# Row loads on one queue, one store on another, and the last inverse step's copies shared differently

## The chip, the cores and the metric

The kernel runs on one core of a Trainium2 chip. The metric is the time of one execution on the device, in microseconds (us), lower being better. Several executions are timed; the figure is their median. One further execution is taken with the hardware profiler and gives the profile and the trace.

The core has five engines that run their own instruction streams: TensorE (PE, matmuls into PSUM; PEld is its weight load), VectorE (DVE), ScalarE (ACT), GpSimd (POOL) and SyncE (SP, which here only issues DMAs). DMAs can be issued by SyncE, ScalarE and GpSimd, each into a queue of its own, in the order of the issuing engine's program. Engines wait for one another, and for DMAs, on semaphores.

## The reference

Two layers of each kind, with residuals. Layer A mixes tokens and channels by a filter in the 2D Fourier domain; layer B is a two-matrix MLP with Mish.

```python
def _A_ref(x, w_r, w_i):                      # x: 1 x 2048 x 1024
    X = rfft2(x.astype(float32)); X = X * (w_r + 1j * w_i)
    return irfft2(X, s=(S, D)).astype(bfloat16)

def _B_ref(x, w1, b1, w2):                    # w1: 1024 x 3584, w2: 3584 x 1024
    h = x @ w1 + b1
    return (h * tanh(softplus(h))) @ w2

x = x + _A_ref(_layernorm(x), A_w_r, A_w_i)
x = x + _B_ref(_layernorm(x), B_w1, B_b1, B_w2)
x = x + _A_ref(_layernorm(x), A_w_r, A_w_i)
x = x + _B_ref(_layernorm(x), B_w1, B_b1, B_w2)
```

## The kernel before

The program is written out by hand: Python functions append instructions to one list per engine, in the order in which they are called, and a small tracker adds the semaphore waits that reads and writes of named resources demand. There is no planner: the order of the calls is the order of each engine's work, and an instruction that waits holds back everything behind it on its engine.

x lies in SBUF as XS, 16 tiles of 128 tokens by 1024 channels. Layer A does the Fourier transforms as steps of matmuls with constant tables: two forward steps over short factors (`s1` L626, matmuls L641; `s2` L740, matmuls L748), a third along the tokens (`s3`), the filter's multiplication on VectorE, and back through `i1`, `i2` and `i4`. The work between `s2` and `i2` goes in eight groups g = 0 to 7, interleaved by a written-out order (`order_A`).

**The start.** The prologue loads x twice: as XS, for the statistics of the layer norm, and in another arrangement, XR, which `s1` multiplies. XR is filled by `rows` (L404): for each q of four quarters (32 of 128 positions n1) and each of eight channel blocks h, one DMA of 512 rows of 256 bytes, 128 KB. SyncE issues all of quarters 0 and 2 and the even h of quarters 1 and 3 (24 loads). The odd h of quarter 1 are issued by GpSimd, after a wait for all of quarter 0. The odd h of quarter 3 are issued by ScalarE from `late_rows`, called in `first_scales` (L596) after the statistics. Behind the rows SyncE issues the table FD, which `s2` needs, the small table JT, and then (`open_tables`, `constants`) the first filter weights w_r and w_i, the further tables and M, BD, MT and others. The layer norm's scales are folded into the tables of `s1`: `scaled` (L611) makes 16 scaled tables, on ScalarE for j = 1 (L616), on GpSimd for j = 2, 4, 9, 10, 11 and 13, on VectorE for the rest (L622). `s1` runs 16 groups j of eight matmuls; j waits for quarter j // 4 of XR and for its scaled table; three pairs of PSUM banks take turns; the results are copied to SBUF by ScalarE (L647), and by VectorE for j = 5, 10 and 14 (L649). Then follow `s2` of group 0, the matmuls that mirror the filter's weights (L1039, which wait for JT, w_r and w_i of the group) and VectorE's copies of them (L1050), and `s2` of group 1, part of which VectorE copies (L785).

**The turn through memory.** After `i2` of a group, its result U (512 KB) is stored to a scratch tensor u_d in device memory (`u_turn`, L925) and read back with another arrangement into UT (`u_back`, L949, 2,048 rows of 256 bytes), because `i4` needs the groups interleaved over the partitions. SyncE issues the stores of groups 0 to 6 and the loads. Each load waits for its store. In SyncE's order `u_back(5)` stands before the store of group 6, and `u_back(6)` is issued during group 7. Group 7 is stored in two halves by ScalarE, and read back in four quarters (`u_last`, L955), two by ScalarE and two by SyncE. Meanwhile TensorE does some filler matmuls (`spin`, L658), puts the residual into the banks (`residual_first`, L1067) and does more filler (`hold`, L663: 16 matmuls in the first layer A, 11 in the second).

**The last inverse step.** `i4` (L1072, matmuls L1078) first does the token tiles 0 to 3, in four parts u of 32 channel positions, two banks each. `out_first(u, t, prog)` (L1083) copies the tiles t and t + 1 of part u from PSUM to XS, one instruction of 128 x 512 elements; the line shown for it is that of a helper (L579 on ScalarE, L583 on VectorE). It names its two banks as written, so two copies of the same part are made one after the other. After the copy of t = 0, VectorE takes a quarter of the statistics of tiles 0 and 1 (`stats_quarter`, L488); after u = 3 the quarters are aggregated (L490), and the scale follows (`root`, L448 on ScalarE and L450 on VectorE), the normalized tiles (`apply`, L528), their transposes on TensorE (L1188), copies (L1193) and the first matmuls of layer B (L1227). The order, in `layer_B`:

```python
for u in range(4):
    self.i4(0, 4, 32 * u, 32, 2 * u)
    if u == 0:
        self.hold(2, 7)
    self.out_first(u, 0, act)
    for j in range(2):
        self.stats_quarter(j, u)
    if u == 0:
        self.out_first(0, 2, dve)
```

The copies of t = 2 of u = 1, 2 and 3 follow on ScalarE. Both layers A end this way. Layer B computes its products by a scheme with seven instead of eight block products and takes most of the time (L1267, L1366); the change does not touch it.

Of the kernel before, what the change touches and what calls it, by code (L numbers as in the profile page):

```python
# [7 lines left out]
P = 128  # L8
# [172 lines left out]
class KB:  # L181
# [200 lines left out]
    def prologue(self):  # L382
        sp = self.sp
        self.op(self.pool, lambda e: e.memset(self.EPS[:], 1e-5), writes=[self.r_eps, self.r_warm])
        xt = self.x[0].rearrange("(t p) d -> p t d", p=P)

        for a, b in ((10, 11), (0, 1), (1, 2), (11, 12), (2, 3), (3, 4), (12, 13), (4, 6), (13, 14), (6, 8), (14, 15), (8, 10), (15, 16)):
            self.dma(self.act if a == 10 else sp, self.XS[:, a:b, :], xt[:, a:b, :], f"x{a}", writes=self.r_xs[a:b])
        self.warm(ACT.Sqrt)
        small = {}  # L390
        def load_small(name, n, d):
            b = self.alloc(name, self.o[name], [n], d)
            self.dma(sp, b.ap, self.con[name], name.lower(), writes=[b.res])
            small[name] = b
        load_small("M0", P, BF)
        load_small("IDF", P, F32)
        self.M0, self.IDF = small["M0"], small["IDF"]

        self.XR = self.alloc("XR", self.o["XR"], [P, P])
        self.r_xr = []  # L400
        xv = self.x[0].rearrange("(n2 n1) (h l) -> h n2 n1 l", n2=16, l=P)
        self.r_xr = [Res(f"xr{q}") for q in range(4)]

        def rows(q, h, prog):  # L404
            self.dma(prog, self.XR.ap[h:P:8, 32 * q:32 * q + 32, :], xv[h][:, 32 * q:32 * q + 32, :], f"xr{q}{prog.name}",
                     parts=[self.r_xr[q]], reads=self.r_xr[:1] if prog is self.pool else [])
        for q in range(4):
            for h in range(8):
                if h % 2 == 0 or q not in (1, 3):
                    rows(q, h, sp)  # L410
                elif q == 1:
                    rows(q, h, self.pool)
        self.late_rows = lambda: [rows(3, h, self.act) for h in (1, 3, 5, 7)]
        self.dma(sp, self.FD[:], self.con["FD"], "fd", writes=[self.r_fd])
        load_small("JT", 4 * P, BF)
        self.JT, self.r_jt = small["JT"].ap, small["JT"].res
        self.w1_next = 0
# [168 lines left out]
    def first_scales(self):  # L586


        dve, act = self.dve, self.act
        for j in range(10):  # L590
            self.stats_dve(j)
        for j in range(10, 16):
            self.stats_act(j)
        self.sums_to_mv(10, 6)
        self.root(0, 16)
        self.late_rows()  # L596
        rt = self.alloc("RT", self.o["RT"], [16, 8], F32)
        self.op(dve, lambda e: e.tensor_copy(rt.ap, self.RS[:, 2, :].unsqueeze(2).to_broadcast([P, 16, 8])),
                reads=self.r_rs, writes=[rt.res])
        bank = self.r_bank[7]  # L600
        self.group([lambda e: e.transpose(self.PS[:, 7, 0:P], rt.ap.rearrange("p a b -> p (a b)"), self.IDF.ap)],
                   reads=[rt.res, self.IDF.res], writes=[bank])
        self.op(dve, lambda e: e.tensor_copy(rt.ap.rearrange("p a b -> p (a b)"), self.PS[:, 7, 0:P]), reads=[bank], writes=[rt.res])
        self.MN = self.alloc("MN", self.o["MN"], [P, P])
        self.r_mn = [Res(f"mn{j}") for j in range(16)]
        for r in self.r_mn:
            r.inherit(self.MN.res)
            r.begin()
        self.RT = rt
# [108 lines left out]
    def layer_A(self, li):  # L718
# [7 lines left out]
        dve, act, sp, pool = self.dve, self.act, self.sp, self.pool  # L726
# [198 lines left out]
        def u_turn(g, half):  # L925

            u = U[g % 3]
            if g == 7:
                h = slice(8 * half, 8 * half + 8)
                if half == 0:  # L930
                    u_back(6)
                self.dma(act, self.u_d[g][:, h, :], u.ap[:, h, :], f"uwh{half}", reads=[u.res], writes=[self.r_ud7[half]])
                if half:
                    u_last()
            elif half:
                if g == 6:
                    u_back(5)
                self.dma(sp, self.u_d[g], u.ap, f"uw{g % 3}", reads=[u.res], writes=[self.r_ud[g]])
                if 0 < g < 6:
                    u_back(g - 1)  # L940

# [7 lines left out]
        def u_back(g):  # L949
            if self.UT is None:  # L950
                open_ut()
            self.dma(sp, self.UT.ap[g:P:8, :, :], self.u_d[g].rearrange("l r n -> r l n"), f"usp{g % 3}",
                     reads=[self.r_ud[g]], parts=self.r_ut)

        def u_last():  # L955

            for q in range(4):
                l = slice(32 * q, 32 * q + 32)
                self.dma((act, act, sp, sp)[q], self.UT.ap[7:P:8, l, :], self.u_d[7][l, :, :].rearrange("l r n -> r l n"),
                         f"ul{q}", reads=self.r_ud7, parts=self.r_ut[q:q + 1])  # L960
# [17 lines left out]
        for stage, g, h in self.order_A():  # L978
            if stage == 2:
                s2(g, h)  # L980
                if li == 0 and h == (g < 2):
                    filter_bins(g)
                    if g in (0, 1):
                        load_w(g + 5)
                    elif g == 4:
                        load_w(7)
            elif stage == 3:
                s3(g, h)
                if h:
                    if 1 <= g < 6:  # L990
                        load_tabs(g + 2)
                    if li == 0:
                        self.keep_filter(g)
                    elif g < 4:
                        load_w(g + 4)
            elif stage == 4:
                i1(g, h)
                if h and g < 6:
                    load_btabs(g + 2)
            else:  # L1000
                i2(g, h)
                u_turn(g, h)
# [77 lines left out]
                                               stop=lo > 0 or l % k == k - 1))  # L1080
        self.group(fns, reads=self.r_ut[u0 // 32:(u0 + n - 1) // 32 + 1] + [self.r_mt], writes=self.r_bank[bank:bank - (-n // k)])

    def out_first(self, u, t, prog):  # L1083

        b = slice(2 * u, 2 * u + 2)
        src = self.PS[:, b, :].rearrange("p b (i c) -> p c b i", c=32)[:, 8 * t:8 * t + 16]
        dst = self.XS[:, t:t + 2, :].rearrange("p n (h l) -> p (n h) l", l=P)[:, :, 32 * u:32 * u + 32]

        self.copy(prog, dst.rearrange("p c (b i) -> p c b i", i=16), src, [], self.r_bank[b], parts=self.r_xs[t:t + 2])

    def i4_out(self, lo, nb, u0, n, bank, staged, r_staged, prog):

# [71 lines left out]
    def layer_B(self, li, last):  # L1164
        pe, dve, act, sp, pool = self.pe, self.dve, self.act, self.sp, self.pool
# [331 lines left out]
        def staged_rest(bank, n):  # L1497

            u0 = self.u0
            self.u0 += n  # L1500
            self.i4(4, 12, u0, n, bank)
            return lambda: self.i4_out(4, 12, u0, n, bank, YS, r_ys, act)
# [11 lines left out]
        for u in range(4):  # L1514
            self.i4(0, 4, 32 * u, 32, 2 * u)
            if u == 0:
                self.hold(2, 7)
            self.out_first(u, 0, act)
            for j in range(2):
                self.stats_quarter(j, u)  # L1520
            if u == 0:
                self.out_first(0, 2, dve)
        rests = [staged_rest(0, 10)]
        for u in range(1, 3):
            self.out_first(u, 2, act)
# [294 lines left out]
```

## Time and profile before

| | us |
|---|---|
| median of 4 runs | 928.47 (926.64 to 930.53) |
| profiled execution, whole | 929.72 |
| its span, first to last instruction | 927.9 |
| TensorE busy in the span | 873.7 (94%) |
| VectorE busy | 622.5 (67%) |
| ScalarE busy | 435.2 (47%) |
| GpSimd busy | 151.8 (16%) |
| start of `s1`'s first matmul / of `s2`'s | 23.07 / 40.71 |
| start of `i4` in the first and the second layer A | 113.37 / 563.24 |
| start of layer B's first matmul (L1227), first and second | 122.30 / 572.17 |

All times inside an execution are counted from the start of the span. The granted TensorE clock was 1.000. In the profile's lines, an engine's name with a q (SPq, ACTq) is the engine issuing a DMA or waiting; XS, ARENA and PS are SBUF and PSUM, in_A_x_dram is x in device memory, u_scratch is u_d; ARENA holds XR, UT and all other working tiles. The chain of waits goes back from the last instruction, at each step to what released it; an engine's time that is not on it is hidden behind something else. "Idle before" in a timeline is the time for which the engine stood still ahead of an instruction, with what ended it.

### The profile page before, as it was taken

To read this page: it belongs to the slowest core of one execution; us is meant where nothing else is said; L and a number is where in the kernel's file an instruction comes from. 1 tells how busy PE (TensorE), PEld (TensorE's weight loads), DVE (VectorE), ACT (ScalarE), POOL (GpSimd) and SP (SyncE) were. 2 spreads that over 40 slices of the span, in tenths; PEclk is the share of its full clock that TensorE was granted. 3 is DMA by queue.
4 is the path that set the end of the run, shared out by engine and by line. 5 is a ranking of instruction groups with operands and counts; after the bars stand their busy time and mean duration, and the time that the engine had idled before them with its cause. 6 is when DMAs were issued, how large, how long until landed. Compare 5 with 4: busy or idle time off the path is not lost.

```text
span 927.9 us, 13543 instructions
## 1 busy us (share of the span) xinstructions
PE 873.7 (94%) x5426; PEld 470.9 (51%) x5503; DVE 622.5 (67%) x995; ACT 435.2 (47%) x645; POOL 151.8 (16%) x174
## 2 busy tenths in 40 slices
PE   0799889999999999999998988999999999999998
PEld 0677576444444444444446766754444444444443
DVE  7699368687789567558857775666747655554473
ACT  6899485456213385520009975757550015552000
POOL 0833003960003642010121200000000000000000
DMA  8979871674786388364732786445166635732432
GB/s 251 277 259 274 229 190 59 228 278 116 283 257 241 142 306 305 131 215 151 276 104 84 231 223 160 149 160 172 46 194 190 201 131 191 276 120 85 170 124 110
DMA packets 151711, 175.99 MB, mean 190 GB/s; under 512 B 73080, under 2 KB 130648, under 8 KB 151528
## 3 DMA queue, kind: packets, MB, share of 16 engines
q1 hardware_dynamic: 136160, 129.27, 44.7%
q0 software_dynamic: 10224, 43.42, 12.6%
q10 hardware_dynamic: 5264, 2.43, 1.0%
q8 instruction: 43, 0.70, 0.3%
q14 instruction: 20, 0.16, 0.1%
HBM read 130.78 MB, written 40.89 MB: 185 GB/s over the span
## 4 chain that ended last, share of the span: by engine, by line
PE 82%; DVE 6%; DMA 4%; ACT 3%; SPq 2%; POOL 2%; issue 1%; ACTq 0%; DVEq 0%; POOLq 0%
PE PS L1366 34%; PE PS L1267 29%; PE PS L1227 6%; PE PS L748 3%; PE PS L849 2%; SPq L251 2%; PE PS L879 2%; PE PS L1078 2%; DMA ARENA<-in_B_w_dram 2%; POOL ARENA L1160 1%; DMA ARENA<-in_A_x_dram 1%; PE PS L1188 1%; ACT ARENA L647 1%; ACT ARENA L457 1%; PE PS L911 1%
## 5 line engine op out<-in xcount | busy, mean ns | idle before, releaser
L1366 PE MATMUL PS<-ARENA 128*128 128x512 bf16 x1535 | 338.3, 379 | 2.0 <-DMA ARENA<-in_B_w_dram 0.2
L1267 PE MATMUL PS<-ARENA 128*128 128x512 f16 (+1 forms) x1265 | 279.1, 379 | 2.3 <-DVE ARENA L1272 0.8
L1366 PEld LDWEIGHTS PS<-ARENA 128*128 128x128 bf16 x1568 | 153.3, 98 | 185.0 <-DVE ARENA L1409 0.7
L1272 DVE TENSOR_TENSOR ARENA<-PS,ARENA 128x512 f32<-128x512 f32 x230 | 157.1, 691 | 101.0 <-PE PS L1267 92.5
L1267 PEld LDWEIGHTS PS<-ARENA 128*128 128x128 bf16 x1288 | 125.3, 98 | 153.7 <-DVE ARENA L1272 3.5
L1277 ACT ACTIVATE ARENA<-ARENA,B 128x512 bf16<-128x512 f32 x138 | 98.8, 721 | 69.6 <-DVE ARENA L1272 64.2
L579 ACT ACTIVATE ARENA<-PS 128x512 f32<-128x512 f32 (+3 forms) x86 | 61.6, 726 | 111.0 <-PE PS L1267 92.9
L1160 POOL TENSOR_TENSOR ARENA<-ARENA 128x512 bf16<-128x512 bf16 x56 | 72.0, 1286 | 75.1 <-DVE ARENA L528 60.9
L457 ACT ACTIVATE ARENA<-XS 128x1024 bf16<-128x1024 bf16 x60 | 63.2, 1053 | 36.8 <-DVE XS L1417 33.0
L1227 PE MATMUL PS<-ARENA 128*128 128x256 bf16 (+1 forms) x524 | 73.2, 295 | 3.6 <-DVE ARENA L1193 1.9
L1391 DVE TENSOR_TENSOR ARENA<-ARENA 128x3584 bf16<-128x3584 bf16 x32 | 63.9, 2017 | 0.0
L1417 DVE TENSOR_TENSOR XS<-PS,ARENA 128x512 bf16<-128x512 f32 x52 | 35.8, 690 | 39.8 <-PE PS L1366 39.5
L1227 PEld LDWEIGHTS PS<-ARENA 128*128 128x128 bf16 x528 | 50.3, 98 | 22.3 <-DVE ARENA L1193 3.3
L1409 DVE TENSOR_TENSOR ARENA<-PS,ARENA 128x512 f32<-128x512 f32 x48 | 32.9, 688 | 28.1 <-PE PS L1366 27.7
L1231 ACT ACTIVATE ARENA<-PS,B 128x256 bf16<-128x256 f32 (+1 forms) x66 | 33.0, 514 | 29.0 <-PE PS L1227 28.8
L1277 ACT ACTIVATE ARENA<-PS,B 128x512 bf16<-128x512 f32 x46 | 31.5, 685 | 18.4 <-PE PS L1267 18.4
L1405 DVE TENSOR_TENSOR ARENA<-ARENA,XS 128x512 f32<-128x512 f32 x52 | 36.8, 731 | 0.5
L448 ACT ACTIVATE RS<-MV,EPS 128x1 f32<-128x1 f32 (+2 forms) x11 | 3.2, 295 | 71.6 <-DVE MV L570 70.1
L849 PE MATMUL PS<-ARENA 128*128 128x256 bf16 x256 | 32.7, 273 | 1.3 <-DVE ARENA L814 1.0
L748 PE MATMUL PS<-FD,ARENA 128*128 128x256 bf16 (+1 forms) x256 | 31.4, 271 | 2.5 <-ACT ARENA L647 1.3
L805 ACT ACTIVATE ARENA<-PS 128x1024 bf16<-128x1024 f32 x30 | 30.4, 1046 | 5.0 <-PE PS L796 5.0
L476 DVE BATCH_NORM_STATS2 BN<-XS 128x6 f32<-128x512 bf16 x44 | 27.6, 668 | 5.4 <-DMA XS<-in_A_x_dram 5.4
(103 smaller groups left out, 807.1 us busy)
## 6 DMA issues: line engine op xcount, KB each, us to landing
ARENA<-in_B_w_dram SPq DMA_DIRECT2D x30, 896.0 KB, 6.7
ARENA<-w1s_scratch SPq DMA_DIRECT2D x28, 896.0 KB, 4.7
ARENA<-w2s_scratch SPq DMA_DIRECT2D x24, 896.0 KB, 6.4
w1s_scratch<-ARENA POOLq DMA_DIRECT2D x14, 896.0 KB, 4.4
ARENA<-in_B_w_dram SPq DMA_DIRECT2D x24, 512.0 KB, 4.4
u_scratch<-ARENA SPq DMA_DIRECT2D x14, 512.0 KB, 4.4
ARENA<-u_scratch SPq DMA_DIRECT2D x14, 512.0 KB, 5.9
w2s_scratch<-ARENA POOLq DMA_DIRECT2D x8, 896.0 KB, 4.1
```

The lines of the kernel that those rows point to most:

```text
L457: self.op(act, lambda e, i=i, f=f: e.activation(junk.ap, x, f, accum_out=sums[:, i:i + 1]), reads=[self.r_xs[j]], writes=[junk.res], parts ...
L579: fn = (lambda e: e.activation(dst, src, ACT.Copy)) if scale is None else \
L748: fns.append(lambda e: e.matmul(dst, at(r), FD[:, t:t + n], start=start, stop=stop))
L849: fns.append(lambda e, c=c, part=part: e.matmul(ps[:, c * 256:(c + 1) * 256], yk.ap[:, part, c * P:(c + 1) * P], t[:, (128, 0)[part]:(384, ...
L1160: self.op(self.pool, lambda e, dst=A(dst), x=A(x), y=A(y), op=op: e.tensor_tensor(dst, x, y, op), reads=[b.res] + list(after), writes=[b.rs])
L1227: fns.append(lambda e, db=db, bank=bank, fl=fl: e.matmul(PS[:, bank, 0:w], wb.ap[:, db, fl * P:(fl + 1) * P], x.ap[:, db, tok], start=(db ...
L1267: self.group([lambda e, db=db: e.matmul(PS[:, bank, :], A[:, db, :], mov[:, db, :], start=(start and db == 0), stop=(db == 3), skip_group_ ...
L1272: self.op(dve, lambda e: e.tensor_tensor(dst.ap, PS[:, bank, :], x.ap, ALU.add), reads=[self.r_bank[bank], x.res], writes=[dst.res])
L1277: self.op(act, lambda e: e.activation(at, src, ACT.Mish, bias=self.B1[:, ft:ft + 1]), reads=[res, self.r_b1], writes=[ra])
L1366: self.group([lambda e, i=i, k=k, b=PB[n][k].ap: e.matmul(PS[:, bank, :], ap[:, i, t * P:(t + 1) * P], b[:, i - 7 * k, :], start=(start an ...
L1391: self.op(dve, lambda e: e.tensor_tensor(ap[dst][:, f, :], ap[x][:, f, :], ap[y][:, f, :], op), reads=part(x, k) + part(y, k), writes=part ...
L1405: self.op(dve, lambda e: e.tensor_tensor(a[t], a[t], x, ALU.add), reads=[rx], writes=[r[t]])
```

## The change

Three places. First, all rows of XR are issued by SyncE: eight DMAs of 256 KB for quarters 0 and 1 together, which now count as one resource, then eight of 128 KB for quarter 2 and eight for quarter 3; `late_rows` and GpSimd's loads are gone. Second, the store of group 6 in `u_turn` is issued by ScalarE. Third, `out_first` takes a number of tiles n. For u = 3 ScalarE copies tile 0 alone and VectorE then tile 1 alone, ahead of the statistics in VectorE's order; and copy (0, 2) is made by ScalarE instead of VectorE.

```diff
         xv = self.x[0].rearrange("(n2 n1) (h l) -> h n2 n1 l", n2=16, l=P)
-        self.r_xr = [Res(f"xr{q}") for q in range(4)]
-
-        def rows(q, h, prog):
-            self.dma(prog, self.XR.ap[h:P:8, 32 * q:32 * q + 32, :], xv[h][:, 32 * q:32 * q + 32, :], f"xr{q}{prog.name}",
-                     parts=[self.r_xr[q]], reads=self.r_xr[:1] if prog is self.pool else [])
-        for q in range(4):
+        for q, n in ((0, 2), (2, 1), (3, 1)):
+            r = Res(f"xr{q}")
             for h in range(8):
-                if h % 2 == 0 or q not in (1, 3):
-                    rows(q, h, sp)
-                elif q == 1:
-                    rows(q, h, self.pool)
-        self.late_rows = lambda: [rows(3, h, self.act) for h in (1, 3, 5, 7)]
+                s = slice(32 * q, 32 * (q + n))
+                self.dma(sp, self.XR.ap[h:P:8, s, :], xv[h][:, s, :], f"xr{q}", parts=[r])
+            self.r_xr += [r] * n
...
         self.root(0, 16)
-        self.late_rows()
...
                 if g == 6:
                     u_back(5)
-                self.dma(sp, self.u_d[g], u.ap, f"uw{g % 3}", reads=[u.res], writes=[self.r_ud[g]])
+                self.dma(act if g == 6 else sp, self.u_d[g], u.ap, f"uw{g % 3}", reads=[u.res], writes=[self.r_ud[g]])
...
-    def out_first(self, u, t, prog):
+    def out_first(self, u, t, prog, n=2):
         b = slice(2 * u, 2 * u + 2)
-        src = self.PS[:, b, :].rearrange("p b (i c) -> p c b i", c=32)[:, 8 * t:8 * t + 16]
-        dst = self.XS[:, t:t + 2, :].rearrange("p n (h l) -> p (n h) l", l=P)[:, :, 32 * u:32 * u + 32]
-        self.copy(prog, dst.rearrange("p c (b i) -> p c b i", i=16), src, [], self.r_bank[b], parts=self.r_xs[t:t + 2])
+        src = self.PS[:, b, :].rearrange("p b (i c) -> p c b i", c=32)[:, 8 * t:8 * t + 8 * n]
+        dst = self.XS[:, t:t + n, :].rearrange("p n (h l) -> p (n h) l", l=P)[:, :, 32 * u:32 * u + 32]
+        self.copy(prog, dst.rearrange("p c (b i) -> p c b i", i=16), src, [], self.r_bank[b], parts=self.r_xs[t:t + n])
...
-            self.out_first(u, 0, act)
+            if u < 3:
+                self.out_first(u, 0, act)
+            else:
+                self.out_first(u, 0, act, 1)
+                self.out_first(u, 1, dve, 1)
             for j in range(2):
                 self.stats_quarter(j, u)
             if u == 0:
-                self.out_first(0, 2, dve)
+                self.out_first(0, 2, act)
```

## The prediction

> **What bounds the kernel now.** I read the page first: its busy table and its chain of work that ended last.
>
> ```profile
> span 927.9 us, 13543 instructions
> PE 873.7 (94%) x5426; PEld 470.9 (51%) x5503; DVE 622.5 (67%) x995; ACT 435.2 (47%) x645; POOL 151.8 (16%) x174
> PE 82%; DVE 6%; DMA 4%; ACT 3%; SPq 2%; POOL 2%; issue 1%; ACTq 0%; DVEq 0%; POOLq 0%
> ```
>
> TensorE carries the chain. What is left to the others, some 18%, includes the three places of this change: the start, and the end of each layer A. So second I asked for the chain in order of time there. The start:
>
> ```profile
> 12.00 4.34 SPq L251
> ...
> 17.15 0.63 SPq L251
> ...
> 18.49 3.00 DMA ARENA<-in_A_x_dram
> ...
> 21.79 1.40 POOL ARENA L251 x2
> ...
> 23.82 6.07 DMA ARENA<-in_A_x_dram
> ...
> 29.99 2.73 PE PS L641 x24
> ...
> 40.71 1.69 PE PS L748 x16
> ...
> 44.65 1.22 DVE ARENA L785
> ```
>
> Columns: start, us, what. Quarter 0 of the rows lands at 18.49 + 3.00 = 21.50. GpSimd waits for it, issues its four loads of quarter 1, and the last of them lands at 23.82 + 6.07 = 29.9; the first step's second quarter (L641) starts at 29.99. The second step (L748) starts at 40.71.
>
> Third, DMA by stretch (last column GB/s):
>
> ```profile
> 15.00:17.00 2.00, 0.00 (x0) 0.00 (x0) 1.93 (x6) 1.71 (x4) 0.00 (x0) 1.00 0.26 41
> 17.00:21.00 4.00, 0.05 (x1) 0.05 (x1) 3.35 (x11) 2.60 (x5) 0.00 (x0) 1.00 0.80 182
> 21.00:30.00 9.00, 4.36 (x34) 3.33 (x35) 7.07 (x7) 6.31 (x12) 8.11 (x7) 1.00 1.03 247
> ```
>
> SyncE alone moved rows at 182; three queues together moved 247. Fourth, the end of the second layer A, from the chain:
>
> ```profile
> 558.31 4.80 DMA ARENA<-u_scratch
> ...
> 563.24 0.95 PE PS L1078 x32
> ...
> 567.06 0.61 ACT XS L579
> 567.69 0.44 DVE BN L488
> ```
>
> TensorE finished its filler and stood 0.53 us (timeline) before the last inverse step (L1078). In the first layer A it did not: there filler runs to 113.53 and L1078 follows.
>
> **Part 1, the rows.** Removed: four issues on GpSimd (2.66 us, L251), four on ScalarE (2.73 us). Eight loads of double size (1,024 packets of 256 B) replace eight and eight; SyncE issues 24 loads as before, but 4 MB instead of 3 MB.
>
> SyncE's issue: an unhindered 512-packet load takes 0.63 + 0.04 = 0.67 us. A 1,024-packet one is not in the trace. From below 0.67, if length costs nothing. From the nearest larger row:
>
> ```profile
> 551.79 1.37 SPq L251 DMA_DIRECT2D u_scratch<-ARENA  x1
> 557.01 0.53 SPq L251 DMA_DIRECT2D ARENA<-u_scratch  x1
> ```
>
> A 2,048-packet load costs 0.53 and holds back the store behind it, which took 1.37 against 0.33 elsewhere; together 1.94, so 0.97 for half. From above, 2 x 0.67 = 1.34. I take 0.95, by the 2,048-packet row, as its packets are the same. The 4.34 us stall ends at 16.35, with two double loads' worth issued; I keep it. Six more and 16 single ones: 16.35 + 6 x 0.95 + 16 x 0.67 = 32.8, against 33.15 now. What SyncE issues next (FD, the filter's first weights, tables) moves 0.35 earlier. Outer bound: 24 loads' worth after 21.5 at the 182 GB/s above: 3.15 MB take 17.3 us, to 38.8, where the trace's completion records put the last SyncE row at 35.6: 3.2 later.
>
> Landing of quarters 0 and 1: between 21.5 and 29.9 sixteen loads landed, 0.525 each. Eight more after 21.5 is 25.7, less 0.6 because the first eight need not wait for 0.67 issues: 25.1. So the step's first matmul moves from 23.07 to about 25.2; that is lost, but the hole before 29.99 goes. From there ScalarE decides: 13 copies (L647) of 1.02 us, 0.93 apart, after 0.9 us of matmul: 25.2 + 0.9 + 12 x 0.93 + 1.02 = 38.3, against 40.62. VectorE keeps up: its copy of group 10 comes near 33, the scaled tables 14 and 15 (L622, 1.13 each) follow by 36.5, when group 15 can first have its banks. Quarter 3, needed near 35, lands 2.4 after its last issue (as quarter 0 did: 19.1 to 21.5), at 35.2. So the step ends 2.3 us earlier.
>
> What is late next: FD, 39.3 now (33.19 + 6.1 by the DMA view), hence 38.95; and the filter's w_i, 41.42 now (VectorE's wait before L1050 ends there), hence 41.1, for the filter matmul that stands at 42.25 in TensorE's order. So of 2.3 us only 42.25 - 41.1 = 1.15 gets through. **Part 1: -1.2 us**; ends -2.3 (weights in time) and +2.4 (3.2 late, less the 0.83 that w_i has to spare). Behind it VectorE runs without a gap from 44.65 to 62, so the shift is kept.
>
> A rule to weigh. The rows: 182 GB/s on one queue, 247 on three. The Trainium skill, DMA: Bandwidth & Descriptors, section "Issuing engines are not separate DMA queues", says that issuing from more engines saves only the sequencer's issue time, as all share the same 16 engines; by that rule the 182 is SyncE's issue, double loads lift it, and part 1 is -1.2; by the rows taken as a limit of one queue it is +2.4. The rows speak for the rule in one place: two `u_back` loads queued on SyncE alone landed 2.1 us apart (completion records), 512 KB each, 250 GB/s.
>
> **Part 2, group 6's store.** On SyncE it stands behind `u_back(5)`, is issued at 551.79 and has landed at 557.01, when `u_back(6)`, which waits for it, is issued. ScalarE's own stores, half as long, land in 2.6 us (DMA view). On ScalarE it can go at 551.2, after the copies that fill it (L923). Behind it in ScalarE's order is the copy of 551.11 (L579): wait and issue cost 0.06 + 0.33 + 0.05, as its own store at 554.8 shows, so that copy ends near 552.2; the next starts at 552.31 after 0.60 idle. That idle is the cover; without it up to 0.4 of each layer's end is lost. The last loads of UT then have less before them: in the first layer they land 3.2 us after issue (109.93 to 113.1), not 4.80. TensorE can gain its 0.53 wait and no more; in the first layer nothing, as filler binds. **Part 2: -0.5**, ends -0.5 and 0.
>
> **Part 3, the copies.** Copy (0, 2), 0.67 on VectorE (115.66), becomes 0.60 on ScalarE, which is idle 0.63 there: nothing. VectorE's next, the statistics of 116.25, waits for ScalarE's copy of 116.19 anyway, so nothing is won. For u = 3 ScalarE copies half and VectorE the other half, one after the other, as both name the same two banks as written. ScalarE's half ends near 117.6, but VectorE comes to its own only after the statistics of u = 2 (end 117.78). Half a copy is not in the trace: VectorE 128x128 from PSUM 0.29, 128x512 0.67; by the line between them 0.42, at least 0.29, at most 0.67. Statistics start overlapping its end by 0.09: 117.70 + 0.42 - 0.09 = 118.03 instead of 117.82. ScalarE's gain has no taker: the waiting engine is VectorE. Everything up to the first matmul of layer B (root, apply, transposes) follows. **Part 3: +0.2 in each layer, +0.4**; ends +0.1 and +1.0.
>
> **Sum.** -1.2 - 0.5 + 0.4 = -1.3 us. The profiled execution took 929.72 (span 927.9 and 1.8 around): it becomes 928.4. It lies 1.25 above the median of 928.47, so I forecast a median of 927.2.
>
> **Rivals.** One queue is slower than three, in SyncE's queue from 21.5 us: it decides once quarter 3 lands more than 0.83 after 35.6, that is, below some 210 GB/s. At 182: +2.4 - 0.5 + 0.4 = +2.3, 930.8; at 165 the rows take 19.1 us, 5.0 late, less 0.8: +4.2, in all +4.1, 932.6. For it: every stretch of SyncE alone on rows shows about 182. Against: those issued 128 KB per 0.67 us, no faster.
> Part 1 does nothing: the later start eats the closed hole, or SyncE's end does not move and 42.25 stays, being TensorE's own order: 0 - 0.5 + 0.4 = -0.1, 928.4.
> The whole lead gets through: weights land early because the engines have less backlog, and part 3 costs its least: -2.3 - 0.5 + 0.1 = -2.7, 925.8. The 41 GB/s hole at 15 to 17 us, if longer loads fill it, adds up to 0.6.
>
> **Chances.** About 0.3% (2.8 us) is what a measurement of this kernel tells from no change. Forecast 0.45 (all within). Part 1 nothing 0.19 (within). One queue slower 0.20, most beyond 0.3%: 0.18 slower, 0.02 within. Whole lead 0.16, counted as faster beyond 0.3% with the filled hole. Together faster 0.16, same 0.66, slower 0.18. The range reaches from 924.8 (whole lead with the hole filled, less runs' scatter) to 931.6 (the slow queue near 175 GB/s).
>
> **What would show it.** Right: L641 starts near 25 and runs without the hole, L748 near 39, L785 near 43.5; GpSimd starts its tables near 22; no wait before L1078 in the second layer; statistics of u = 3 0.2 later after L1078 ends. Wrong: SyncE issues FD after 34, or L785 after 44.65; a gap in ScalarE's copies near 552.3; statistics of u = 3 no later.

## The result, and the profile after

The changed kernel takes 932.32 us (median of 32 runs, 928.94 to 936.13) against 927.31 for the kernel before beside it (53 runs): ratio 1.005, interval 1.004 to 1.006. It is 5.0 us slower; 1.3 faster was forecast.

The profiled execution took 935.77 us, 3.45 above that median, so it shows more than the usual loss. From its page, busy time and the shares of the chain:

```profile
span 933.9 us, 13535 instructions
PE 878.6 (94%) x5426; PEld 475.0 (51%) x5503; DVE 622.8 (67%) x995; ACT 436.5 (47%) x647; POOL 147.4 (16%) x170
PE 85%; DVE 6%; SPq 3%; ACT 3%; DMA 2%; issue 1%; ACTq 0%; DVEq 0%
```

TensorE runs the same 5,426 matmuls and is busy 4.9 us longer (873.7 before): the matmuls themselves became slower. In the table of stretches the column behind POOL's is the granted TensorE clock, the last one GB/s:

```profile
15.00:17.00 2.00, 0.00 (x0) 0.00 (x0) 1.93 (x5) 1.88 (x5) 0.00 (x0) 1.00 1.32 205
17.00:21.00 4.00, 0.42 (x1) 0.18 (x1) 2.44 (x9) 2.31 (x5) 0.00 (x0) 1.00 1.30 214
21.00:30.00 9.00, 5.65 (x57) 5.29 (x56) 7.64 (x8) 6.99 (x13) 8.45 (x5) 1.00 1.13 206
38.00:42.00 4.00, 2.84 (x26) 2.52 (x24) 2.31 (x3) 2.94 (x3) 1.19 (x1) 0.50 1.04 335
126.00:131.00 5.00, 4.21 (x26) 2.89 (x24) 4.60 (x13) 2.89 (x5) 0.00 (x0) 0.50 1.03 269
```

Two of these stretches in the profile of before:

```profile
38.00:42.00 4.00, 2.33 (x28) 1.89 (x26) 2.57 (x3) 2.50 (x4) 2.15 (x3) 1.00 0.90 285
126.00:131.00 5.00, 4.99 (x77) 4.46 (x75) 3.01 (x8) 4.23 (x7) 0.00 (x0) 1.00 0.45 132
```

The clock is halved in `s2` and at the start of the first layer B; the trace's clock records put the halving at 35.8 for 10.2 us and at 124.5 for 6.8 us. The profile of before had no such stretch. The 41 GB/s hole at 15 to 17 is not in this profile.

Line numbers of the changed kernel lie 6 or 7 below those of before (L641 is L634, L748 is L741, L1078 is L1071, L1188 is L1181, L1227 is L1220). The chain at the start:

```profile
14.22 1.21 SPq L251
...
20.32 1.22 SPq L251
21.59 0.64 SPq L251
...
31.50 5.37 DMA ARENA<-in_A_x_dram
...
36.91 2.75 PE PS L634 x24
...
41.66 3.15 PE PS L741 x16
```

The first 1,024-packet load, issued at 7.71, holds SyncE 0.69 us. From 14.22 to 20.32 each issue behind such a load holds it 1.08 to 1.22, and so does that of the first 512-packet load (20.32); an issue behind a 512-packet load takes 0.63 or 0.64 (one 1.11). SyncE is through with the rows at 32.12 (33.15 before, 32.8 forecast), but the last load of quarter 3 lands at 36.86; TensorE stands 3.34 us before L634, and what follows runs at half clock: 16 matmuls take 3.15 us, against 1.69. The end of the first layer A, from TensorE's timeline:

```profile
117.47 0.95 PE L1071 MATMUL PS<-MT,ARENA 128*128 128x32 bf16 x32 [1.02 <-DMA ARENA<-u_scratch]
...
124.58 1.89 PE L1181 MATMUL PS<-IDENT,ARENA 128*128 128x128 bf16 x16 [1.27 <-DVE ARENA L522]
```

The same places in before:

```profile
113.37 0.95 PE L1078 MATMUL PS<-MT,ARENA 128*128 128x32 bf16 x32
...
120.30 1.08 PE L1188 MATMUL PS<-IDENT,ARENA 128*128 128x128 bf16 x16 [0.88 <-DVE ARENA L528]
```

A wait of 1.02 us for UT where before had none, 1.27 instead of 0.88 before the transposes, and these at half clock: 1.89 instead of 1.08.

### The profile page after: what moved, and what is told of

Same layout as the page of the kernel before. It is cut to its first block, busy times and chain, and to the rows that moved or that the text cites. A ratio compares the mean times of both kernels' runs of the same rounds, so it can differ in the third digit from the quotient of the medians.

```text
span 933.9 us, 13535 instructions
## 1 busy us (share of the span) xinstructions
PE 878.6 (94%) x5426; PEld 475.0 (51%) x5503; DVE 622.8 (67%) x995; ACT 436.5 (47%) x647; POOL 147.4 (16%) x170
## 4 chain that ended last, share of the span: by engine, by line
PE 85%; DVE 6%; SPq 3%; ACT 3%; DMA 2%; issue 1%; ACTq 0%; DVEq 0%
PE PS L1359 36%; PE PS L1260 29%; PE PS L1220 6%; SPq L251 3%; PE PS L741 3%; PE PS L842 2%; PE PS L872 2%; PE PS L1071 2%; PE PS L1181 1%; ACT ARENA L451 1%; PE PS L904 1%; DVE ARENA L800 1%; PE PS L787 1%; ACT ARENA L640 1%; DMA u_scratch<-ARENA 1%
## 5 line engine op out<-in xcount | busy, mean ns | idle before, releaser
L1220 PE MATMUL PS<-ARENA 128*128 128x256 bf16 (+1 forms) x524 | 74.9, 299 | 3.5 <-DVE ARENA L1186 1.7
L1220 PEld LDWEIGHTS PS<-ARENA 128*128 128x128 bf16 x528 | 51.0, 99 | 23.0 <-DVE ARENA L1186 3.3
L741 PE MATMUL PS<-FD,ARENA 128*128 128x256 bf16 (+1 forms) x256 | 33.2, 281 | 2.5 <-ACT ARENA L640 1.3
L1235 DVE TENSOR_TENSOR ARENA<-ARENA 128x2048 f16<-128x2048 bf16 x16 | 25.3, 1582 | 9.0 <-PE PS L1220 8.7
```

The costliest lines, as they stand in the source:

```text
L741: fns.append(lambda e: e.matmul(dst, at(r), FD[:, t:t + n], start=start, stop=stop))
L1220: fns.append(lambda e, db=db, bank=bank, fl=fl: e.matmul(PS[:, bank, 0:w], wb.ap[:, db, fl * P:(fl + 1) * P], x.ap[:, db, tok], start=(db ...
```

## Experiments

Each kernel was timed in five rounds against the kernel before on the same chip; "over before" is the difference of the medians. The interval of a ratio is plus or minus 0.0012 to 0.0020, that is 1.1 to 1.9 us. I first took the parts one by one, with the theory that one queue for the rows is what costs.

**Part 1 alone** (the diff's first and second hunk).

> Only the rows are changed (part 1). Theory: the rows carry most of the loss, since the last SyncE load lands after TensorE has run out of work, TensorE stands still for some 3 us, and its granted clock then drops to half for the second step: 2.5 to 4 us slower than before, granted clock under 1.000, the second step's first 16 matmuls at about 3 us instead of 1.7. Rival (the store of group 6 carries the loss): 0 to 1 us slower, clock 1.000.

Measured 927.46 us, ratio 0.9995 (0.9982 to 1.0008), mean granted clock 0.9990. Not slower: the theory fell.

**Part 2 alone.**

```diff
-                self.dma(sp, self.u_d[g], u.ap, f"uw{g % 3}", reads=[u.res], writes=[self.r_ud[g]])
+                self.dma(act if g == 6 else sp, self.u_d[g], u.ap, f"uw{g % 3}", reads=[u.res], writes=[self.r_ud[g]])
```

> Only the store of group 6 is moved to ScalarE (part 2). Theory: it gains 0.5 us in the second layer A and loses up to 1.2 us in the first, where the read of group 6 now runs beside the stores of group 7 and delays the last one: within 1 us of before. Rival (the store carries the loss, through a wait before the last inverse step that halves the clock at the start of layer B): 2 to 4 us slower, with a granted clock of one half around 120 to 130 us.

Measured 928.56, ratio 1.0012 (0.9999 to 1.0026); 0.6 over before. Its mean clock was 0.9980, with 3 of 12 runs at 1.000 (19 of 34 of before in the same job). In its profile the clock is halved at 562.2 for 3.4 us, and TensorE stands 1.63 us for UT just ahead of that:

```profile
561.17 0.95 PE L1078 MATMUL PS<-MT,ARENA 128*128 128x32 bf16 x32 [1.63 <-DMA ARENA<-u_scratch]
```

**Part 3 alone** (`out_first` with n, and the two copies).

> Only the copies are shared anew (part 3). Theory, as predicted: VectorE's half copy of 0.41 us stands ahead of the last statistics, +0.2 us in each layer, +0.4 us in all, clock 1.000. Rival: the longer wait of TensorE before layer B halves its clock, 1 to 2 us slower.

Measured 930.69, ratio 1.0026 (1.0008 to 1.0044), 2.75 over before, where 0.4 was expected. Its mean clock was 0.9966, and only 3 of 12 runs were at 1.000 (before: 80 of 156 in all jobs, mean 0.9987). Those three have a median of 927.26, 0.3 above before's runs at 1.000 in the same job (926.97). So what is beyond the direct cost goes with the clock.

**Filler in the prologue.** The whole change, and 14 matmuls ahead of `s1`'s group 12:

```diff
+            if not li and j == 12:
+                self.group([lambda e: e.matmul(self.PS[:, 6, :], self.M0.ap, self.MN.ap[:, 0:4, :].rearrange("p a b -> p (a b)"),
+                                               start=True, stop=True)] * 14,
+                           reads=[self.M0.res, self.r_mn[0]], writes=[self.r_bank[6]])
```

> The changed kernel, with 14 more matmuls of 128x512 on data already in SBUF, into a free bank, ahead of the first step's group 12, where TensorE waits for the last rows. They compute nothing that is used. Theory (the halved clock is what the late rows cost): the clock stays full through the second step, and some 2 us of the loss come back, 929 to 931 us. Rival (the lateness of the rows themselves costs the time): no gain, or slower by what the matmuls outlast the wait.

Measured 931.37, 3.4 over before, ratio 1.004 (1.0026 to 1.0055). That misses the 929 to 931 of its theory by a little, and the interval reaches into it: at most a part of the loss lies there.

**The clock at the start of layer B.** The theory now was the rival of `copies`: part 3 lengthens TensorE's idle time there, and the clock is halved more often. Nine matmuls fill that time:

```diff
         self.out_first(3, 2, act)
+        self.hold(5, 4)
         for f in rests:
             f()
...
             transposed(0, j, xn[j])
+        self.spin(4, 1)
         self.warm(ACT.Mish)
```

> Part 3 alone, with nine matmuls of 128x512 put into TensorE's idle time at the start of each layer B (five adding zero to bank 4 ahead of the transposes, four into the free bank 1 behind them); what they compute is not used. Clock theory (part 3's cost is the halved clock that follows from TensorE's longer idle time): the run comes back to before plus the 0.4 us that the copies cost directly, 928.2 to 929.0, the mean granted clock of the runs 0.9985 or more, and no half clock window at the first product L1227. Rival (the copies cost time through the longer path of VectorE and ScalarE alone): it stays at 930.2 to 931.2, as part 3 alone did (930.69), or higher by what the added matmuls delay.

Measured 927.41, ratio 0.9987 (0.9973 to 1.0002); mean clock 0.9995. The timelines of TensorE, first `copies`, then `copies_hold`:

```profile
119.05 1.46 PE L1188 MATMUL PS<-IDENT,ARENA 128*128 128x128 bf16 x16 [1.27 <-DVE ARENA L528]
121.30 3.60 PE L1227 MATMUL PS<-ARENA 128*128 128x256 bf16 x16 [0.79 <-DVE ARENA L1193]
```

```profile
118.83 1.03 PE L663 MATMUL PS<-BD,ARENA 128*128 128x512 bf16 x4
120.05 1.08 PE L1188 MATMUL PS<-IDENT,ARENA 128*128 128x128 bf16 x16 [0.19 <-DVE ARENA L528]
120.96 1.03 PE L658 MATMUL PS<-BD 128*128 128x512 bf16 x4
122.05 1.92 PE L1227 MATMUL PS<-ARENA 128*128 128x256 bf16 x16
```

The sixteen first matmuls of layer B take 3.60 us in one and 1.92 in the other, with the same copies ahead of them. What part 3 lost beyond its direct cost was the clock. In the twenty profiles of all kernels the clock is halved at the start of a layer B in `after`, `copies`, `idle1` and `idle4`, which lengthen the wait, not in `warm`, which does too, and in none of the eleven with the nine matmuls. What a halving costs: from the second layer B's first matmul to the last matmul 17 profiles take 352.81 to 352.83 us, and the three with the clock halved there 354.33 to 354.48.

> The kernel before, with the same nine matmuls at the start of each layer B; what they compute is not used. Clock theory: before's runs at a clock of 0.998 and 0.996 (15 of 34, 928.6 and 930.3 against 927.0 at 1.000) owe it to the same stretch, so most of them rise to 1.000 and the median falls to 927.0 to 927.5. Rival (the half clock windows of before come from elsewhere, or the added matmuls stand in the way): 927.9 or more.

Measured 927.40, ratio 0.9987 (0.9973 to 1.0001), 11 of 12 runs at a clock of 1.000. So before itself seems to lose a little there, though the interval just reaches no change. The direct cost of the copies does not show between these two kernels (927.41 and 927.40 in one job); the intervals could hide it.

The other direction, idle time alone, with the copies left as they were (`idle1`: one more aggregate, `idle4`: four more):

```diff
-            t = self.op(self.dve, lambda e: e.bn_aggr(self.MV[:, j, :], bn), reads=[r], writes=[r])
+            for _ in range(2 if j else 1):
+                t = self.op(self.dve, lambda e: e.bn_aggr(self.MV[:, j, :], bn), reads=[r], writes=[r])
```

> The kernel before, with one more aggregate (L490, 0.19 us, the same values a second time) ahead of the scale in each layer B: TensorE's idle time ahead of the transposes grows by 0.19 us, as under part 3, with the copies left as they were. Clock theory with a threshold in the length of the idle time: as part 3 alone, 929.5 to 931.2 and a mean clock near 0.9965. Rival (it is not the length but the new arrangement of the copies): 0.4 us over before, 928.0 to 928.7, and before's clock, 0.9985 or more.

> The kernel before, with four more aggregates (0.77 us) ahead of the scale in each layer B. Direct cost 2 x 0.77 = 1.5 us, 929.5, if that is all; the clock theory adds a half clock window of 3.4 us (1.7 to 2 us lost) to each layer in most runs: 931.5 to 933.5, mean clock 0.996 or less.

Measured 930.60 (ratio 1.0019, 1.0004 to 1.0033; mean clock 0.9959) and 934.23 (1.005, 1.003 to 1.007; 6 runs, mean clock 0.9932, none at 1.000). 0.19 us of VectorE's time in each layer costs 2.4 us (0.4 to 3.1 by the interval), as much as the new copies did: it is the length of the idle time, not the arrangement. Four times as much cost 6.0, more than forecast. By the slope of time against clock given below, 750 us for each unit, the lower clock makes up 1.9 and 4.0 of these, and the added aggregates themselves 0.4 and 1.5. TensorE's timeline of `idle1` in the second layer (its line numbers lie one above those of before):

```profile
568.34 1.08 PE L1189 MATMUL PS<-IDENT,ARENA 128*128 128x128 bf16 x16 [1.17 <-DVE ARENA L529]
570.34 3.58 PE L1228 MATMUL PS<-ARENA 128*128 128x256 bf16 x16 [0.93 <-DVE ARENA L1194]
```

**What else is in the whole change.**

> The whole change, with the nine matmuls at the start of each layer B; what they compute is not used. If part 3's loss is the clock there, and nothing else is new when the parts come together, the change falls from 5.0 us over before to the sum of the others: part 1 -0.5, part 2 +0.6, copies with the matmuls -0.8, so 927.0 to 928.5. If the parts cost more together than alone (the first layer's end and the clock in the prologue, as the profile of the whole change shows), 929 to 930.5. Rival (the clock at layer B has no part in the whole change): 932.

Measured 929.99, ratio 1.002 (1.0008 to 1.0032), mean clock 0.9992: half of the 5.0 us is gone, 2.4 is left. That is what the clock explains: (0.9992 - 0.9958) x 750 = 2.6.

> As after_hold, with group 6 stored from ScalarE in the second layer only, and from SyncE in the first as before. If the store costs in the first layer (profile of the change: group 7's second half landed 4.1 us later, TensorE waited 1.02 us before L1071) and gains 0.5 in the second, this is 0.9 to 1.7 us below after_hold. Rival (the first layer's wait in that profile came from the prologue's lateness or by chance): equal to after_hold within 0.4 us.

(`act if g == 6 and li else sp`.) Measured 928.45, 0.9 over before, ratio 1.0011 (0.9997 to 1.0024): 1.5 below `after_hold`. That points to a cost of part 2 in the first layer, where I had put nothing; the intervals of the two overlap, and the table below shows it better.

> Parts 1 and 2 without part 3 (the copies as before, no added matmuls). If the parts add, before -0.5 +0.6, 927.5 to 928.7. If parts 1 and 2 together bring what neither does alone, 929 to 931, with TensorE's wait before the first layer's L1078 near 1 us and a lower mean clock than 0.998.

Measured 930.85, ratio 1.0028 (1.0012 to 1.0044), mean clock 0.9983: above the sum.

> What the runs so far point to as the fastest: part 1, part 2 in the second layer only, the copies as before, and the nine matmuls at the start of each layer B, whose results are not used. Sum: part 1 -0.5, the matmuls -0.8, part 2 in the second layer -0.5: 926.0 to 926.8 where before is 928. Rival (the gains are those of the clock alone and rows or store give nothing): 927.2 to 927.6, as the matmuls alone gave.

Measured 928.43, ratio 1.0008 (0.9994 to 1.0021). No gain: with the clock held, part 1 and the second layer's store give nothing.

**Part 2's mechanism.** From the trace's completion records of twenty profiles (all kernels; the two that hold the read back, below, are left out of the column on ScalarE), counted from the issue of group 7's second half:

| | store of 6 on SyncE | on ScalarE |
|---|---|---|
| store of group 6 landed (second layer, mean) | +1.24 | -0.97 |
| `u_back(6)` issued (second layer, mean) | +1.26 | -0.95 |
| second half landed, first layer | 4.19 to 4.74, mean 4.41 (11) | 3.71 to 5.74, mean 5.01 (7) |
| second half landed, second layer | 2.15 to 2.98, mean 2.48 (9) | 3.44 to 4.94, mean 4.47 (9) |
| `i4` starts, first layer | mean 8.06 | mean 8.70 |
| `i4` starts, second layer | mean 7.19 | mean 7.96 |

The store of group 6 lands 2.2 us earlier, as meant, and `u_back(6)` is issued 2.2 us earlier. That puts its 2,048 small packets ahead of the store of group 7's second half instead of behind it. The last loads (`u_last`) are issued when that half has landed, and `i4` waits for them: 0.64 later in the first layer, 0.77 in the second. The test leaves the store on ScalarE and holds only the read back:

```diff
                 if half == 0:
-                    u_back(6)
                 self.dma(act, self.u_d[g][:, h, :], u.ap[:, h, :], f"uwh{half}", reads=[u.res], writes=[self.r_ud7[half]])
+                if half == 0:
+                    u_back(6, [self.r_ud7[0]])
...
-        def u_back(g):
+        def u_back(g, after=()):
...
-                     reads=[self.r_ud[g]], parts=self.r_ut)
+                     reads=[self.r_ud[g]] + list(after), parts=self.r_ut)
```

> Part 1 alone, with the nine matmuls at the start of each layer B, whose results are not used. If part 1 gives nothing and costs nothing on the path (mean start of the second step L748 in the six profiles with part 1 39.5, in the seven without 39.1; the program's end 0.30 later), this is the matmuls' 927.4 plus 0 to 0.7: 927.2 to 928.2. If part 1 gains what was predicted, 926.2. If parts 1 and 2 do cost more together than apart (parts 1 and 2 together were 3.3 above before, alone -0.5 and +0.6), part 1 alone shows none of it here; if part 1 carries that cost, 928.5 to 929.5.

> Part 2 alone, with the same nine matmuls. Theory: with group 6 stored from ScalarE, the read back of group 6 is issued 1.5 to 3 us earlier and runs beside the store of group 7's second half, which lands later (second layer 3.4 to 4.8 us after its issue instead of 2.2 to 3.0; first layer 4.7 to 5.5 instead of 4.2 to 4.7), and the last loads, issued on that landing, go later with it: about 0.7 in each layer, 1.0 to 1.6 in all, 928.4 to 929.2. Rival (part 2 alone is as harmless as its run without the matmuls seemed, +0.6): 927.6 to 928.2.

> As store_hold, but the read back of group 6, which SyncE issues, also waits for the landing of group 7's first half, so that it is issued 1.5 to 2.3 us after the second half's store. Theory (the read back beside the second half is the cost): the second half lands as in before (second layer 2.2 to 3.0 after its issue, first layer 4.2 to 4.7), and the time is that of the matmuls alone, 927.2 to 927.9. Rival (the cost is the store's place on ScalarE's queue itself): as store_hold.

> The kernel before with the nine matmuls at the start of each layer B a second time: the version that the runs so far point to as faster than both. Theory: 0.7 to 1.1 below before, mean clock 0.9995 or more. Rival (the first run was chance): no less than 0.3 below.

Measured in one job: `rows_hold` 927.69 (ratio 0.9989, 0.9977 to 1.0001), `store_hold` 928.81 (1.0006, 0.999 to 1.0022), `store_late_hold` 928.53 (1.0, 0.9986 to 1.0014), `hold_again` 927.62 (0.9987, 0.9972 to 1.0002). The DMA view, cut to the moment of the second half's issue in the second layer (last number: us from issue to landing), of before, `store_hold` and `store_late_hold`:

```profile
u_scratch<-ARENA ACTq DMA_DIRECT2D x1, 256.0 KB, 2.4
```

```profile
u_scratch<-ARENA ACTq DMA_DIRECT2D x1, 256.0 KB, 4.6
```

```profile
u_scratch<-ARENA ACTq DMA_DIRECT2D x1, 256.0 KB, 2.5
```

The same store from the same queue takes 2.4, 4.6 and 2.5 us, as the read back is behind it, ahead of it, and behind it again; in the first layer 4.2, 5.7 and 4.2. `i4` follows: 7.38, 8.00 and 7.31 after the issue. That is the mechanism, as far as the landing and the start of `i4` go. The medians agree only in part: part 2 costs 1.2 us (`store_hold` less `hold_again`), and holding the read back gave 0.3 of it, which the intervals cannot tell from all or from nothing.

**Do the parts add?**

> Parts 1 and 2 with the nine matmuls at the start of each layer B, whose results are not used. If the parts add once the clock is held (part 1 +0.1, part 2 +1.2 against the matmuls alone), 0.4 us over before, 928.0 to 929.0 where before is 928. If parts 1 and 2 bring something together that neither does alone, as their run without the matmuls suggests, 929.5 to 930.5.

> The whole change with both causes taken away: the nine matmuls at the start of each layer B, whose results are not used, and the read back of group 6 held until group 7's first half has landed. If the halved clock and the read back are all that the change costs, it comes to the matmuls alone, 0.8 below before, 927.2 to 928.0. If something else is left, it stays between there and after_hold's 2.4 over before, and the profile says in which stage.

Measured 929.32 (ratio 1.0015, 0.9999 to 1.0032) and 928.79 (1.0005, 0.9992 to 1.0018). The whole change with both repairs is 1.1 us over before and 3.9 below the change as it was made. By the terms below, 0.9 and -0.1 over before would be expected (1.61 and 1.08 measured). The same holds for the other kernels with part 1 and something else: each is 0.2 to 1.5 above its sum, about within its interval, but all to the same side. What that is stays open.

## Why the prediction was wrong, point by point

Two steps failed and one term was mis-sized. The clock was put at nothing. Part 2 was to make the last loads of UT earlier and made them later. Part 1's gain was counted from one late profile.

| term | predicted | measured |
|---|---|---|
| part 1 | -1.2 | 0.06 in the start of `s2`, +0.30 at the program's end |
| part 2 | -0.5 | 0.64 + 0.77 = +1.4 |
| part 3, directly | +0.4 | 2 x 0.18 = +0.36 |
| the clock | not in the sum | (0.9987 - 0.9958) x 750 = +2.2 |
| sum | -1.3 | +4.3, of 5.0 |

750 us for each unit of mean clock is the slope of time against clock over the 156 runs of before beside the experiments, and 0.9987 their mean; 0.9958 is the mean of 33 runs of the changed kernel. Some 0.7 us has no term.

**Part 1** was mis-sized by its base. I forecast `s2` near 39 and subtracted from 40.71. Over twenty profiles `s2` starts at 38.45 to 40.71 without part 1 (ten, mean 39.44) and at 38.58 to 41.66 with it (ten, mean 39.51); each mean is uncertain by some 0.3. The one profile I had was the latest of its ten, and the 41 GB/s hole that I meant to close comes and goes with the execution: at 15 to 17 us the other nine profiles without part 1 show 30 in `store_late_hold`, 149 and 156 in two, and 192 to 218 in six; with part 1 two show 72 and 82, and eight 191 to 209. The closed hole before the second quarter was real (L634 starts at 24.38 and runs on), and the time went to the wait for quarter 3. The issue of a double load, put at 0.95, was 0.69 for the first and 1.08 to 1.22 behind another, and yet the sum for SyncE's end came near (32.12 for 32.8). Of the signs named, L634's start near 25 (24.38) and GpSimd's tables near 22 (21.55) came; `s2` near 39 and L785 near 43.5 did not in this profile (41.66, and 47.68 for L778). Of the signs against, L785 after 44.65 came, FD issued after 34 did not (32.16).

The rival of a slow queue did not come at its price: from 15 to 30 us the changed kernel moved (2 x 205 + 4 x 214 + 9 x 206) / 15 = 208 GB/s on one queue, not 182, and `hold_again` 212 on three. But from 21 to 30, where the loads of all three queues are under way, the ten profiles without part 1 show 222 to 263 (mean 236) and the ten with it 205 to 217 (mean 210), and the last row lands 0.5 us later with it (means 35.07 and 34.53). On one queue a 128 KB load went out every 0.67 us, which is 196 GB/s. So a limit by SyncE's issue fits these numbers, as in the rule weighed in the prediction from the Trainium skill (DMA: Bandwidth & Descriptors, "Issuing engines are not separate DMA queues"); no run separates it from a limit of the queue.

The 0.30 at the end stands in all ten profiles with part 1 and in none of the others: it lies between GpSimd's last two semaphore events, 0.38 to 0.40 instead of 0.08 us apart. Why was not tried.

**Part 2** failed at the sentence "The last loads of UT then have less before them". I followed `u_back(6)`, which did come earlier, and took the landing of group 7's second half as given. The last loads wait for that half, and it now had the read back's packets beside it. The words "in the first layer nothing, as filler binds" held only as long as UT was not later. The profile of after shows the second layer as predicted (0.51 gained); over nine profiles that was one early draw. The longer wait feeds the clock term too: in `store` and `store_hold` the clock is halved at 562.2 and 116.0, around `i4`, behind waits of 1.63 and 1.52 us for UT.

**Part 3** was right in every step that it named: VectorE's half copy took 0.41 (0.42 forecast), and the time from `i4` to layer B's first matmul grew from 8.93 to 9.11 in the second layer. What failed is the step to the sum, that 0.2 us on VectorE's chain costs 0.2 us. TensorE waits out that chain with little to do. In the 3.41 us before layer B's first matmul (second layer, by TensorE's timeline) matmuls take 0.53 + 1.08 = 1.61 us in before, 47%; 0.24 + 1.08 = 1.32 in `idle1`, 39%; 0.13 + 1.08 = 1.21 in `copies`, 35%. The runs at a clock of 1.000 are 80 of 156, 2 of 12 and 3 of 12. Before was already at the edge, and the row "granted clock 1.00" of one profile hid that half of its runs were below it. The prediction put the clock at nothing and did not name it as a rival.

The chip's rows show halvings of 3.4, 6.8 and 10.2 us. The Trainium skill (TensorE: Matmul & The Clock Gate, "The HAM clock gate (the "warmup" mystery)") has the clock decided over free-running windows of about 3.4 us, which agrees with these lengths and with the same code meeting it in some runs only. It has the clock drop after an idle window and its section "HAM oscillation — how this bites in real kernels" warns of gaps above about 3.4 us. Here the measurement goes further. In each of the 19 profiles with clock records the ends of the halvings lie multiples of 3.41 us apart. Take the spans in windows on that grid. In the window just ahead of each of the 15 halvings inside the spans TensorE is busy for 27 to 55% of the time. Eight windows of 43 to 53% were not followed by a halving, and neither was any of the 4,911 windows at full clock above 55.5%. So no window without matmuls is needed: at the start of layer B in `copies` and `idle1` no gap is above 1.27 us.

The result lies outside the range, on the side of a rival that was wrong in its mechanism.

## What to carry to other kernels

Where a change lengthens a wait of TensorE, count the share of matmul time in 3.4 us around it, not only the wait: near a half, 0.2 us on another engine cost 1.2 here (2.4 in two layers), and a handful of matmuls whose results nobody reads won it back. The kernel before with the nine matmuls is also among the fastest found: 927.40 and 927.62 in two jobs, each 0.13% below before, with intervals that just reach no change (`copies_hold` and `rows_hold` are level with it). When a transfer is made earlier, look for what it now runs beside, and whether the last transfer, not this one, is what is waited for; and take a base from more than one profile where a stretch is ruled by DMAs.

## What was not expected of the hardware

How long the issue of a strided load holds SyncE went here with what was issued ahead of it, not with its own packets: 0.69 us for the first load of 1,024, 1.08 to 1.22 behind such a load for one of 1,024 and for one of 512 alike, 0.63 or 0.64 behind one of 512 (rows of 256 bytes). Over the ten profiles with part 1 the issues behind a 1,024-packet load take 0.81 to 1.52. A store of 256 KB lands in 2.4 us or in 4.6, by whether 2,048 packets of 256 bytes were issued 1 us ahead of it or behind it, from another queue. The prologue of unchanged code starts `s2` anywhere in 2.3 us from one profile to the next.
